# Spectral filter and squared-ReLU FFN: row means taken out in the residual sum, and an FFN norm without them

## The chip, the core and the metric

One core of one Trainium2 chip runs the whole program. The engines have their own instruction queues: TensorE (PE) multiplies, VectorE (DVE) and ScalarE (ACT) do elementwise work and move results from PSUM to SBUF, GpSimd (POOL) has a few jobs at the start, and SyncE (SP) issues most of the DMAs. The metric is the device time of one launch in microseconds; lower is better.

## The reference

The input is x of 2048 rows by 448 columns, in bf16. Two kinds of layer alternate, each twice:

```python
def _A_ref(x, w_r, w_i):                     # spectral filter
    X = rfft2(x.astype(float32))             # over the 2048 rows and 448 columns
    return irfft2(X * (w_r + 1j * w_i), s=(S, D)).astype(bfloat16)
def _B_ref(x, w1, b1, w2, b2):               # FFN, 448 -> 1792 -> 448
    r = maximum(x @ w1 + b1, 0)
    return (r * r) @ w2 + b2
x = A_x
x = x + _A_ref(layernorm(x), A_w_r, A_w_i)
x = x + _B_ref(layernorm(x), B_w1, B_b1, B_w2, B_b2)
x = x + _A_ref(layernorm(x), A_w_r, A_w_i)
x = x + _B_ref(layernorm(x), B_w1, B_b1, B_w2, B_b2)
```

The layer norm subtracts the row's mean and divides by sqrt(variance + 1e-5); it has no scale or offset of its own.

## The kernel before

**Tiles.** x stays in SBUF (`x_sb`, bf16) as 16 tiles of 128 rows. Weights and DFT matrices are loaded once. PSUM has eight banks of 512 fp32 columns; a tile of the program uses one bank or two neighbouring ones.

**The order of the work.** A planner (`_Sched`) collects all operations with their dependences, takes an order for each engine that is written out by hand as lists of operation numbers (`ORDER`), and sets the semaphores. Costs in the planner (such as `(n + 61) / 1.2` ns for an eviction on ACT) matter only where the order leaves a choice. `EV` says which engines may do an eviction. Where PE would stand still, the planner puts in filler matmuls on a matrix of ones (`warm_mm`, L1352).

**First spectral layer.** For each tile: row statistics on DVE or ACT, `rstd` (L865), then a DFT matrix scaled by rstd (`Fs`, L712 on POOL or DVE) and five matmuls (`first_A`), with one eviction into `XA`. Half of the input is first copied on POOL with a shift (`VT<-xin`, L701). Then `spectral`, in eight blocks p: `stage_TD` (matmuls on XA), `stage_B` (matmuls with G), `stage_W` (the complex multiply by the filter: chains of tensor_tensor on DVE, L729), and `stage_Bi` (matmuls with H, evicted into `VT` in single banks, two a block). After that `ffn` begins with the last step of the inverse transform: `stage_TI` (VT by TI, evicted to `tmp` as one instruction a group of one or two tiles) and `stage_AI` (tmp by FI), whose result is added to the residual by a scalar_tensor_tensor (STT, L1104): PSUM times 1.0 plus x, with the row's sum as a second output (`accum_out`).

**FFN norm.** `ln_B` squares x on ACT with a row sum (L1128). From the sum and the sum of squares come mean and variance by small DVE operations. Tiles 0 to 3 go into the FFN unnormalised: x is transposed (tiles 0 and 1 by matmuls with the flip matrix J, `flip`; 2 and 3 by a DMA transpose), and beside the 448 columns of x there are eight auxiliary columns: standard deviation and mean of the row, each as two bf16 parts (`cp` L733, `tt` L729). Their partners are extra rows of W1: b1 and minus the column sums of W1 over 448. So (x - mean) W1 + std b1 comes out of one matmul, relu and square are taken, and the second matmul's result is multiplied by rstd squared (`r2`) when it is added (L1245). Those column sums are made on the chip by `w1_aux` (L806 to L826): 16 matmuls of W1 with ones, an ACT copy scaled by -1/448, an STT for the rest (L820), and three DMAs into rows of W1, with two more for b1. Tiles 4 to 15 (`ln_rows`) are normalised before (`affine`: times rstd, plus -mean rstd, L721 and L722, which wait for small STTs at L1167 and L1171), transposed by DMA, and take b1 as the bias of the relu.

**FFN.** `h_part` and `h_pairs` do the first matmul, relu (ACT) and square (DVE, L729); `o_tile` the second matmul and the STT at L1245, which adds `xb` (x plus b2, a tensor_tensor done before). In the first FFN each finished tile goes on at once to the second spectral layer: `ln_stats` (bn_stats L834, bn_aggr L835), the fold x(d) +- x(447-d) and a second fold on DVE, the subtraction of the mean from one quarter (L738), `second_A` (four matmuls of 128 columns, one eviction to `XA`). The last tile is cut into two halves of 224 columns (`CUT`), the output's last into 336 and 112 (`CUT2`).

**Second spectral layer and second FFN** repeat this with folded matrices; the last STT writes the output tile.

Of the kernel before, what the change touches and what calls it, by code (L numbers as in the profile page):

```python
# [5 lines left out]
ACT = mybir.ActivationFunctionType  # L6
# [5 lines left out]
P = 128  # L12
S = 2048
D = 448
# [10 lines left out]
VB_PAIRS = (2, 3, 4, 5)  # L25

# [9 lines left out]
def make_constants():  # L36
# [88 lines left out]
1384 1389 1394 1399 1410 1404 1407 1413 1416""",  # L125
    "act": """
# [12 lines left out]
1306 1308 1303 1170 1171 1174 1177 1178 1377 1372 1370 1380 1375 1387 1382 1385 1392 1390 1397 1395 1400 1402""",  # L139
    "dve": """  # L140
# [26 lines left out]
    "pool": """  # L167
12 17 14 15 16 20 13 19 22 21 52 60 76 25 105 68 92 84 141 144 23 115 118 24 157 154 18""",
    "sp": """
3 6 4 10 36 8 30 28 41 29 33 32 31 45 34 27 39 37 46 40 44 38 163 35 164 165 166 167 332 355 376 379 378 399 421 442  # L170
401 463 1050 1073 1094 1096 1117 1138 1268 1265 1097 1274 1362 1159 1180 1318 1365 1359 1315 1368 1271 1406 1412 1312
1409 1321 1415 1418""",
}
# [1257 lines left out]
```

## Time and profile before

The runs took 269.94 us (median of three, 269.8 to 269.97).

| | |
|---|---|
| profiled execution | 269.8 us |
| its span | 267.9 us |
| PE busy | 256.9 us, 96% |
| DVE busy | 203.7 us, 76% |
| ACT busy | 175.6 us, 66% |
| POOL busy | 14.9 us, 6% |
| granted PE clock | 1.00 |

PE is busy nearly throughout. A busy PE in the table is a matmul in flight: matmuls overlap, so a row's duration is longer than the time it takes from the next. In the timeline a row is start, duration, engine, line, operation, output and inputs, sizes, count; the bracket at the end is the idle time before it and what ended it.

### The profile page before, as it was taken

Reading aid. Unit: us, or ns where it says so; the run is one execution under the profiler, and the core shown is the slowest. Engines: PE = TensorE matmul, PEld = TensorE weight load, DVE = VectorE, ACT = ScalarE, POOL = GpSimd, SP = SyncE. Lnnn points to the kernel's source line nnn. Section 1 sums busy time; section 2 is a strip of 40 time slices with the busy share of each in tenths; the row PEclk is TensorE's granted clock in tenths of the full one; section 3 lists DMA queues with packets and bytes.
Section 4 is the critical chain, followed back from the end, with each engine's and each line's share of the span. In section 5 each row is a group of like instructions: output and inputs, shape, how many; then the busy total and the mean of one; then the engine's idle time right before and its main releaser. Section 6 shows DMA issues by size and latency. Waiting matters only on the chain.

```text
span 267.9 us, 5691 instructions
## 1 busy us (share of the span) xinstructions
PE 256.9 (96%) x2090; PEld 165.1 (62%) x2090; DVE 203.7 (76%) x724; ACT 175.6 (66%) x393; POOL 14.9 (6%) x31
## 2 busy tenths in 40 slices
PE   8789998999999999999998998899999999999996
PEld 3667587778544555655567766688654675554454
DVE  3978996999999976299997899689995059734442
ACT  5977899987279746784226897899445885040930
POOL 8940000000000000000000000000000000000000
PEclk9999999999999999999999999999999999999999
DMA  7999410022300215000000000001423100023103
GB/s 232 404 291 347 157 40 1 3 40 42 66 10 20 41 22 107 4 0 2 1 0 2 2 0 0 4 14 30 78 60 68 42 0 0 20 39 92 52 0 103
DMA packets 25554, 16.33 MB, mean 61 GB/s; under 512 B 18186, under 2 KB 24566, under 8 KB 25528
## 3 DMA queue, kind: packets, MB, share of 16 engines
q1 hardware_dynamic: 24792, 14.26, 19.7%
q10 hardware_dynamic: 576, 0.92, 0.9%
q0 software_dynamic: 160, 0.81, 0.7%
q8 instruction: 16, 0.26, 0.4%
q14 instruction: 10, 0.08, 0.1%
HBM read 10.46 MB, written 1.84 MB: 46 GB/s over the span
## 4 chain that ended last, share of the span: by engine, by line
PE 76%; DVE 11%; ACT 7%; POOL 2%; issue 2%; DVEq 0%; ACTq 0%; POOLq 0%
PE ps L675 76%; ACT VT L700 4%; DVE tmp L729 4%; DVE arena L729 2%; DVE x_sb L1104 1%; ACT arena L700 1%; POOL Wt L772 1%; DVE x_sb L1245 1%; ACT arena L694 1%; DVE VT L729 1%; ACT XA L700 1%; DVE st L834 1%; POOL VT L701 1%; POOL W_sb L742 1%; ACT VT L1128 0%
## 5 line engine op out<-in xcount | busy, mean ns | idle before, releaser
L675 PE MATMUL ps<-yT,W_sb 64*128 64x512 bf16 (+1 forms) x770 | 90.2, 346 | 0.1
L675 PE MATMUL ps<-W_sb,arena 128*128 128x448 bf16 (+3 forms) x476 | 87.1, 342 | 0.0
L675 PEld LDWEIGHTS ps<-yT,W_sb 64*128 64x128 bf16 (+1 forms) x770 | 56.2, 95 | 30.3 <-ACT arena L694 1.6
L675 PEld LDWEIGHTS ps<-W_sb,arena 128*128 128x128 bf16 x476 | 45.5, 98 | 38.5 <-DVE arena L729 1.6
L729 DVE TENSOR_TENSOR arena<-arena 128x512 bf16<-128x512 bf16 (+1 forms) x140 | 45.2, 365 | 25.3 <-ACT arena L694 24.9
L694 ACT ACTIVATE arena<-ps,b1col 128x512 bf16<-128x512 f32 x84 | 51.7, 692 | 18.1 <-PE ps L675 17.9
L1128 ACT ACTIVATE VT<-x_sb 128x448 bf16<-128x448 bf16 x32 | 18.5, 581 | 22.4 <-DVE x_sb L1104 22.4
L700 ACT ACTIVATE arena<-ps 128x448 bf16<-128x448 f32 (+1 forms) x42 | 26.2, 723 | 6.0 <-PE ps L675 5.9
L1245 DVE SCALAR_TENSOR_TENSOR x_sb<-ps,arena 128x448 bf16<-128x448 f32 (+3 forms) x26 | 14.7, 582 | 12.5 <-PE ps L675 12.2
L694 ACT ACTIVATE mv<-mv,epst 128x1 f32<-128x1 f32 (+1 forms) x41 | 11.7, 296 | 16.9 <-DVE mv L835 10.8
L700 ACT ACTIVATE XA<-ps 128x512 bf16<-128x512 f32 x28 | 15.3, 594 | 6.0 <-PE ps L675 5.9
L694 ACT ACTIVATE arena<-ps 128x256 bf16<-128x256 f32 x56 | 17.8, 400 | 1.3 <-PE ps L675 1.3
L675 PE MATMUL ps<-arena,G_sb 128*128 128x448 bf16 (+1 forms) x84 | 17.0, 335 | 0.4 <-ACT arena L700 0.4
L675 PE MATMUL ps<-H_sb,arena 128*128 128x256 bf16 x128 | 16.2, 273 | 1.2 <-DVE arena L729 0.8
L675 PE MATMUL ps<-yT,VT 64*128 64x512 bf16 x42 | 15.8, 376 | 0.0
L700 ACT ACTIVATE VT<-ps 128x512 bf16<-128x512 f32 (+1 forms) x30 | 14.5, 631 | 1.4 <-PE ps L675 1.4
L729 DVE TENSOR_TENSOR tmp<-arena,Wt 128x896 bf16<-128x896 bf16 x26 | 14.8, 622 | 0.4 <-ACT arena L700 0.4
L675 PEld LDWEIGHTS ps<-H_sb,arena 128*128 128x128 bf16 x128 | 11.9, 98 | 5.1 <-DVE arena L729 3.3
L700 ACT ACTIVATE tmp<-ps 128x896 bf16<-128x896 f32 (+1 forms) x18 | 14.1, 850 | 1.4 <-PE ps L675 1.4
L675 PE MATMUL ps<-TD_sb,XA 112*128 112x112 bf16 (+1 forms) x184 | 13.9, 229 | 1.0 <-ACT XA L700 1.0
L675 PEld LDWEIGHTS ps<-TD_sb,XA 112*128 112x128 bf16 (+1 forms) x184 | 12.3, 98 | 2.8 <-DVE XA L701 1.2
L1104 DVE SCALAR_TENSOR_TENSOR x_sb<-ps,x_sb 128x448 bf16<-128x448 f32 x16 | 9.8, 620 | 4.5 <-PE ps L675 4.5
(89 smaller groups left out, 295.4 us busy)
## 6 DMA issues: line engine op xcount, KB each, us to landing
out_dram<-x_sb SPq DMA_DIRECT2D x15, 112.0 KB, 1.8
W_sb<-in_B_w_dram SPq DMA_DIRECT2D x1, 1568.0 KB, 10.1
W_sb<-in_B_w_dram SPq DMA_DIRECT2D x1, 1344.0 KB, 10.3
xin<-in_A_x_dram ACTq DMA_DIRECT2D x4, 224.0 KB, 4.8
xin<-in_A_x_dram SPq DMA_DIRECT2D x4, 224.0 KB, 4.2
H_sb<-c_H SPq DMA_DIRECT2D x1, 896.0 KB, 9.4
G_sb<-c_G SPq DMA_DIRECT2D x1, 672.0 KB, 7.9
Wt<-in_A_w_i_dram SPq DMA_DIRECT2D x1, 393.8 KB, 7.3
```

Of the source, the lines that this page charges most:

```text
L675: return sch.add("pe", lambda e: e.matmul(_res(o), lhsT, rhs, start=start, stop=stop, skip_group_check=skip), [lhsT, rhs], [o], cost=cost, ...
L694: sch.add("act", lambda e: e.activation(o, _res(i), func, **kw), rd, [o], cost=c)
L700: op = sch.add(engs[0], lambda e: e.activation(o, _res(i), ACT.Copy) if h[0].eng == "act" else e.tensor_copy(o, _res(i)), [i], [o], cost=c ...
L701: e.tensor_copy(o, _res(i)), [i], [o], cost=c[engs[0]], unit=unit)
L729: sch.add(eng, lambda e: e.tensor_tensor(o, _res(a), b, op), [a, b], [o], cost=_free(o) / rate + 69.0)
L742: sch.add(eng, lambda e: e.memset(o, v), [], [o], cost=_free(o) / 1.92 + 60.0)
L772: sch.add("pool", lambda e: e.indirect_dma_start(o, None, (A_w_r, A_w_i)[i], bass.IndirectOffsetOnAxis(ix[:], 0)), [ix[:]], [o], is_dma=Tr ...
L834: small(lambda e, si=si, xi=xi: e.bn_stats(si, xi), [xi], [si], _free(xi) / 0.96 + 69.0)
L1104: small(lambda e, xx=xx, xi=xi, r=r, i=i: e.scalar_tensor_tensor(out=xx, in0=_res(r), scalar=1.0, in1=xi, op0=ALU.mult, op1=ALU.add, accum ...
L1128: sch.add("act", lambda e, i=i, o=o, x=x: e.activation(o, x, ACT.Square, accum_out=sd[:, i, 1:2]), [x], [o, sd[:, i, 1:2]], cost=560.0)
L1245: small(lambda e: e.scalar_tensor_tensor(out=o, in0=_res(i), scalar=r[0] if r else 1.0, in1=xb[:, t, d0:d1], op0=ALU.mult, op1=ALU.add), [ ...
```

## The change

- **Mean in the residual sum.** The STT of `stage_AI` becomes PSUM minus mean plus x, with the mean of the row (known from the layer norm before) as a pointer scalar; it has no row sum any more. A filter of mean-free rows gives mean-free rows, so x in `x_sb` is mean-free after it, and the sum of squares alone gives the variance. Mean of the first norm (`mv`) and of the third (`mv2`, new) are added up into `mv2[..., 3]`, and given back in the last FFN: for tiles 0 to 3 as an STT in place of the tensor_tensor with b2 (`with_b2`), for the others in the STT of `o_tile`, by a pointer.
- **FFN norm.** Mean squared, variance and -mean rstd go. The square root follows the sum of squares. Two auxiliary columns (the standard deviation in two parts) remain of eight; `affine` becomes `scaled` (times rstd alone). `w1_aux` goes with its 16 matmuls and five DMAs; b1 goes twice into W1's extra rows by one DMA.
- **Evictions.** Blocks 1 to 5 of `stage_Bi` (`MERGE`) use two neighbouring banks and one instruction of 1,024 elements. `stage_TI` for tiles 0 and 1 uses two half tiles, evicted by ACT or DVE. The squares of tiles 0 and 1 may be done on DVE.
- **Last tile** of the first FFN: `o_tile` in two halves made of quarters (0, 3) and (1, 2), so that the fold can be done after each; `second_A` in two halves with eight matmuls of 64 columns and two evictions.
- **Order.** Costs of ACT in the planner go from 61 and 112 to 78 and 128, and all of `ORDER` is written anew. Among others, the memset of `x_sb` on POOL moves behind the copies, the b1 matmul moves from the start of the kernel into the first FFN, and for tiles 0 to 3 the second part of h follows the first without output matmuls between. Instructions: PE 2,092 to 2,078, DVE 694 to 652, ACT 361 to 353.

```diff
+MERGE = (1, 2, 3, 4, 5)
...
-        def w1_aux():
-            q = _Tile(1)
-            u = sch.new_unit("pe", 32)
-            for blk in range(4):
-                for i in range(4):
-                    mm(q[lambda b, i=i: ps[32 * i:32 * i + 32, b, 0:D]], ones[:, 0:32], W1_sb[:, blk, D * i:D * (i + 1)],
-                       blk == 0, blk == 3, skip=True, unit=u)
...
         def stage_Bi(p, first):
+                m = _Tile(2) if p in MERGE else None
...
+                if m:
+                    evac(VT[:, :, :, :, 2 * p:2 * p + 2, :].rearrange("p a g t c j -> p (a g t) (c j)"),
+                         m[lambda b: ps[:, b:b + 2, :].rearrange("p a (t c) -> p (a t) c", c=16)], EV["Bi"])
...
         def stage_TI(t, n, late):
+            if n == 1:
+                for g in range(2):
+                    q = _Tile(1)
+                    for r in range(2):
+                        mm(q[lambda b: ps[:, b, 0:HD]], VT[0:QD, r, g, t].rearrange("p c j -> p (c j)"), TI_sb[:, r, g, :],
+                           r == 0, r == 1)
+                    evac(TIo[:, t, g, :], q[lambda b: ps[:, b, 0:HD]], EV["TI1"])
+                return
...
-                small(lambda e, xx=xx, xi=xi, r=r, i=i: e.scalar_tensor_tensor(
-                    out=xx, in0=_res(r), scalar=1.0, in1=xi, op0=ALU.mult, op1=ALU.add, accum_out=sd[:, t + i, 0:1]),
+                m = (mv if first else mv2)[:, t + i, 0:1]
+                small(lambda e, xx=xx, xi=xi, r=r, m=m: e.scalar_tensor_tensor(
+                    out=xx, in0=_res(r), scalar=m, in1=xi, op0=ALU.subtract, op1=ALU.add), [r, xi, m], [xx], 545.0)
...
-            tt(u, a, a, ALU.mult)
...
-            small(lambda e: e.scalar_tensor_tensor(out=u, in0=a, scalar=-1.0 / D, in1=r, op0=ALU.mult,
-                                                   op1=ALU.mult), [a, r], [u])
             for i in range(n):
-                affine(xn[:, i, 0:D], x_sb[:, t + i, 0:D], rstd[:, t + i, 0:1], sd[:, t + i, 2:3], EV["XN"])
+                scaled(xn[:, i, 0:D], x_sb[:, t + i, 0:D], rstd[:, t + i, 0:1], EV["XN"])
...
+        def with_b2(t, n, last):
+            if t < 4 and last:
+                for i in range(t, t + n):
+                    m = mv2[:, i, 3:4]
+                    small(lambda e, i=i, m=m: e.scalar_tensor_tensor(out=xb[:, i, :], in0=x_sb[:, i, 0:D], scalar=m, in1=b2row[:],
+                                                                     op0=ALU.add, op1=ALU.add),
...
+            rs = [r2[:, t, 0:1]] if t < 4 else [mv2[:, t, 3:4]] if last else []
...
-        CUT = ((0, HD), (HD, D)) if HALVES else ((0, D),)
+        CUT = (lambda a: a.rearrange("p (k d) -> p k d", k=4)[:, 0:4:3], lambda a: a[:, QD:3 * QD])
...
+        def fold(t, d0, d1):
+            w = xin[:, t, :].rearrange("p (g d) -> p g d", g=2)
+            a, b = x_sb[:, t, d0:d1], x_sb[:, t, D - 1 - d0:D - 1 - d1:-1]
+            tt(w[:, 0, d0:d1], a, b, ALU.add)
+            tt(w[:, 1, d0:d1], a, b, ALU.subtract)
```

More of the change, by code (lines that the diff above doesn't have):

```diff
@@ L1121, in flip, with ln_B @@
                  EV["T"])
-        def ln_B(t, n):
+        def ln_B(t, n, last):
             for i in range(t, t + n):
@@ L1127, in ln_B @@
                 x = x_sb[:, i, 0:D].rearrange("p (a c) -> p a c", a=4)
[L1128 to L1129 removed]
+                h = []
+                op = sch.add("act", lambda e, i=i, o=o, x=x, h=h: e.activation(o, x, ACT.Square, accum_out=sd[:, i, 1:2])
+                             if h[0].eng == "act" else e.scalar_tensor_tensor(
+                                 out=o, in0=x, scalar=1.0, in1=x, op0=ALU.mult, op1=ALU.mult, accum_out=sd[:, i, 1:2]),
+                             [x], [o, sd[:, i, 1:2]], cost=575.0)
+                h.append(op)
+                if t < NFLIP:
+                    op.alt = {"act": 575.0, "dve": 545.0}
             if t >= 4:
[L1132 removed]
+                ln_rows(t, n, last)
                 return
[L1134 to L1136 removed]
+            b = sd[:, t:t + n, 1]
+            act(b, b, ACT.Sqrt, bias=epst[:, 0:1], scale=1.0 / D)
             if t < NFLIP:
[L1138 to L1149 removed]
+                flip(t, n, 0, 3)
+            aux = x_sb[:, t:t + n, D:D + 2]
+            cp(aux[:, :, 0], b)
+            tt(aux[:, :, 1], b, aux[:, :, 0], ALU.subtract)
             if t < NFLIP:
@@ L1156, in ln_B @@
             sch.tag = "xb" + sch.tag
-            tt(xb[:, t:t + n, :], x_sb[:, t:t + n, 0:D], b2row[:, None, :].to_broadcast([P, n, D]), ALU.add)
+            with_b2(t, n, last)
             small(lambda e: e.reciprocal(rstd[:, t:t + n, 0], b), [b], [rstd[:, t:t + n, 0]])
@@ L1179, in ln_rows @@
             sch.tag = "xb" + sch.tag
-            tt(xb[:, t:t + n, :], x_sb[:, t:t + n, 0:D], b2row[:, None, :].to_broadcast([P, n, D]), ALU.add)
+            with_b2(t, n, last)
             sch.bias += PR["xb"]
@@ L1235, in h_part, with o_tile, r @@
                 tt(hb, hb, hb, ALU.mult)
-        def o_tile(t, d0, d1):
+        def o_tile(t, cut, last):
             hb = hbuf[(t // 4) % 2]
             q = _Tile(1)
+            o, xi = cut(x_sb[:, t, 0:D]), cut(xb[:, t])
+            n = _free(o)
+            def r(a):
+                return a if len(list(o.ap)) == 2 else a.rearrange("p (k d) -> p k d", k=2)
             for fb in range(FB):
-                mm(q[lambda b: ps[:, b, 0:d1 - d0]], hb[:, fb, (t % 4) * P:(t % 4 + 1) * P], W2_sb[:, fb, d0:d1],
+                mm(q[lambda b: r(ps[:, b, 0:n])], hb[:, fb, (t % 4) * P:(t % 4 + 1) * P], cut(W2_sb[:, fb, :]),
                    fb == 0, fb == FB - 1)
-            o, i = x_sb[:, t, d0:d1], q[lambda b: ps[:, b, 0:d1 - d0]]
-            r = [r2[:, t, 0:1]] if t < 4 else []
-            small(lambda e: e.scalar_tensor_tensor(out=o, in0=_res(i), scalar=r[0] if r else 1.0, in1=xb[:, t, d0:d1],
-                                                   op0=ALU.mult, op1=ALU.add),
-                  [i, xb[:, t, d0:d1]] + r, [o], (d1 - d0) / 0.96 + 69.0)
+            i = q[lambda b: r(ps[:, b, 0:n])]
+            rs = [r2[:, t, 0:1]] if t < 4 else [mv2[:, t, 3:4]] if last else []
+            small(lambda e: e.scalar_tensor_tensor(out=o, in0=_res(i), scalar=rs[0] if rs else 1.0, in1=xi,
+                                                   op0=ALU.add if t >= 4 and last else ALU.mult, op1=ALU.add),
+                  [i, xi] + rs, [o], n / 0.96 + 69.0)
         def second_A(t):
@@ L1252, in second_A @@
             scaled(f, FA_sb[:, 0:P], rstd[:, t, 0:1], EV["FS2"])
-            q = _Tile(1)
+            n = 2 if t == NT - 1 else 1
+            q = [_Tile(1) for _ in range(n)]
+            w = P // n
+            u = sch.new_unit("pe")
             for k in range(2):
@@ L1313, in ffn @@
                     sch.bias, sch.tag = 5500.0 * (NT - t), f"o{L}.{t}"
-                    for d0, d1 in ((CUT2 if last else CUT) if t == NT - 1 else ((0, D),)):
-                        o_tile(t, d0, d1)
+                    for k, cut in enumerate((CUT2 if last else CUT) if t == NT - 1 else WHOLE):
+                        o_tile(t, cut, last)
                         if last:
-                            dma("sp", out_dram[:, t, d0:d1], x_sb[:, t, d0:d1])
+                            dma("sp", cut(out_dram[:, t, :]), cut(x_sb[:, t, 0:D]))
+                        elif t == NT - 1:
+                            fold(t, QD * k, QD * (k + 1))
                     if not last:
```

121 lines of the change are left out of this document (52 added, 69 removed), and 92 rows, old and new, of the table ORDER.

## The prediction

> **What bounds the kernel now.** I read the page's head and chain of waits first, then the windows of the stretches in which the chain leaves PE, then the timeline of PE around each of its gaps, with DVE, ACT, POOL and SP beside it.
>
> ```profile
> span 267.9 us, 5691 instructions
> PE 256.9 (96%) x2090; PEld 165.1 (62%) x2090; DVE 203.7 (76%) x724; ACT 175.6 (66%) x393; POOL 14.9 (6%) x31
> PE 76%; DVE 11%; ACT 7%; POOL 2%; issue 2%; DVEq 0%; ACTq 0%; POOLq 0%
> ```
>
> PE is busy for 96% of the span and carries 76% of the chain; DVE has 11%, ACT 7%. So an operation taken off DVE or ACT is worth something only where PE waits for it. Those places are few:
>
> ```profile
> 8.27 0.27 PE L675 MATMUL ps<-Fs,xin 128*128 128x256 bf16 x1 [1.43 <-POOL Fs L712]
> 14.85 0.27 PE L675 MATMUL ps<-Fs,m 128*128 128x256 bf16 x1
> 15.25 0.27 PE L675 MATMUL ps<-Fs,xin 128*128 128x256 bf16 x1
> 33.49 0.94 PE L675 MATMUL ps<-W_sb,ones 128*32 128x448 bf16 x16
> 34.36 0.61 PE L675 MATMUL ps<-H_sb,arena 128*128 128x256 bf16 x4
> 43.04 0.26 PE L675 MATMUL ps<-TI_sb,VT 112*128 112x224 bf16 x1 [0.49 <-DVE VT L701]
> 49.76 0.57 PE L675 MATMUL ps<-TI_sb,VT 112*128 112x112 bf16 x8 [0.43 <-ACT tmp L700]
> 143.86 0.61 PE L675 MATMUL ps<-Fs,tmp 128*128 128x128 bf16 x8 [0.52 <-DVE mv L835]
> 145.09 0.40 PE L675 MATMUL ps<-Fs,tmp 128*128 128x128 bf16 x4 [0.19 <-DVE tmp L738]
> 168.49 0.26 PE L675 MATMUL ps<-TI_sb,VT 112*128 112x224 bf16 x1 [0.46 <-DVE VT L701]
> 168.98 1.60 PE L675 MATMUL ps<-TI_sb,VT 112*128 112x224 bf16 x15 [0.23 <-ACT VT L700]
> 174.38 0.55 PE L675 MATMUL ps<-TI_sb,VT 112*128 112x112 bf16 x8 [0.62 <-DVE x_sb L733]
> ```
>
> The columns are start, duration, engine and line, tile, count, and in brackets the idle time with what ended it. The gaps lie in the start, at the two spectral-to-FFN joins (43 to 50, 168 to 175) and at the FFN-to-spectral join (143 to 146). The two W stretches are a mixed case, shown by their windows (length, then busy time of PE, PEld, DVE, ACT, POOL, granted clock, DMA):
>
> ```profile
> 20.00:42.00 22.00, 21.94 (x182) 15.78 (x180) 20.80 (x40) 19.24 (x36) 0.00 (x0) 1.00 0.51 167
> 149.40:167.00 17.60, 16.09 (x165) 11.80 (x162) 17.25 (x35) 16.08 (x28) 0.00 (x0) 1.00 0.00 1
> ```
>
> In the first W stretch PE and DVE are both full; in the second DVE is (17.25 of 17.60) and PE has 1.5 us of slack. The two FFN bodies (about 51 to 137 and 176 to 265) are PE's alone.
>
> **The change, part by part.**
>
> *Start.* The first real matmul waits for the scaled matrix Fs, made on POOL, and POOL's queue had a memset ahead of it, which now stands later:
>
> ```profile
> 5.85 0.31 POOL L742 MEMSET x_sb<- 128x256 bf16 x1
> 6.11 1.55 POOL L701 COPY VT<-xin 128x448 bf16<-128x448 bf16 x3
> 7.65 1.39 POOL L712 TENSOR_SCALAR Fs<-FA_sb,rstd 128x256 bf16<-128x256 bf16 x3
> ```
>
> Memset to next start is 6.11 - 5.85 = 0.26, so the first Fs can start at 7.39, and PE 0.26 earlier, if the statistics of that tile are there by then; they are DVE work of the first microseconds that is not lengthened. The tiles' order also differs, which can touch the gap of 15.25 - 14.85 - 0.11 = 0.29 (the 0.11 are 256 columns at the pace of the row at 168.98: (1.60 - 0.26)/14 = 0.096 us for 224). I take -0.35; ends 0 (the time is lost again at the stretch's last eviction) and -0.55.
>
> *Sums of W1 (w1_aux).* 16 matmuls go, 34.36 - 33.49 = 0.87 us of PE; so do one eviction on ACT, one STT on DVE and five small DMAs.
>
> ```profile
> 42.85 0.61 DVE L820 SCALAR_TENSOR_TENSOR yT<-ps,yT 128x448 bf16<-128x448 f32 x1
> ```
>
> The STT stands behind the evictions for which PE waits at 43.04, so it gives nothing. The 0.87 lie in the stretch where DVE is busy for 20.80 of 22.00: PE arrives earlier and waits for DVE's chain of complex multiplies. Ends 0 and -0.87; I take -0.05 for this and the new order of the stretch, because DVE's idle 1.2 us there is mostly its first wait and last evictions. What PE loses as cover is idle time, and nothing is queued behind it. On SP, the loads of the inverse DFT's and FFN's weights no longer stand behind the sums' DMAs; PE waits for none of them in the rows above, so 0.
>
> *Two-bank evictions of stage_Bi.* Five pairs a layer become single instructions.
>
> ```profile
> L700 ACT ACTIVATE VT<-ps 128x512 bf16<-128x512 f32 x26 | 13.4, 650 | 1.4 <-PE ps L675 1.4
> L700 ACT ACTIVATE arena<-ps 128x896 bf16<-128x896 f32 x16 | 14.1, 987 | 0.8 <-PE ps L675 0.8
> ```
>
> The slope (987 - 650)/384 = 0.88 ns an element gives 987 + 112 = 1100 ns for 1,024, against 2 x 650: up to 0.2 us of ACT a pair, 1 us a layer. The last pair's eviction starts later, since it waits for both banks, and the TI stage waits for VT by DVE first (0.49, 0.46). ACT is under its window in both W stretches; 0, ends -0.2 and +0.3 per layer.
>
> *First join (43 to 51).* Each residual STT loses its accumulator, and takes a pointer for a scalar in place of 1.0; the variance arithmetic (mean squared, subtraction, product with rstd) goes.
>
> ```profile
> L1245 DVE SCALAR_TENSOR_TENSOR x_sb<-ps,rstd,arena 128x448 bf16<-128x448 f32 x8 | 5.3, 677 | 0.0
> L1245 DVE SCALAR_TENSOR_TENSOR x_sb<-ps,arena 128x448 bf16<-128x448 f32 x22 | 13.2, 619 | 11.0 <-PE ps L675 10.7
> L1167 DVE SCALAR_TENSOR_TENSOR mv<-mv 128x2 f32<-128x2 f32 x12 | 1.8, 154 | 0.9 <-ACT VT L1128 0.7
> ```
>
> The pointer form is 677 - 619 = 58 ns dearer, on 32 STTs 1.9 us of DVE; some 44 small operations go, of which L1167's idle of 0.9 shows that they also waited on ACT. Along the join, PE does the same work, and its gap of 0.43 at 49.76 is an eviction on ACT, now two half ones of which DVE takes most. But the last FFN work on tiles 2 and 3 moves: the second h_part follows the first without the second output tile's matmuls between.
>
> ```profile
> 56.73 1.04 PE L675 MATMUL ps<-yT,W_sb 128*128 128x256 bf16 x8
> 57.60 2.81 PE L675 MATMUL ps<-W_sb,arena 128*128 128x448 bf16 x14
> 60.25 2.02 PE L675 MATMUL ps<-yT,W_sb 128*128 128x256 bf16 x17
> 55.55 1.34 SPq L662 DMA_TRANSPOSE yT<-x_sb  x1
> yT<-x_sb SPq DMA_TRANSPOSE x2, 3.0
> ```
>
> Before, the transpose of tiles 2 and 3 was issued at 55.55 and landed 3.0 later, and PE needed it at 60.25. Without the 14 output matmuls it is needed by about 57. By my count of what goes ahead of it, about nine small operations at some 0.15 in DVE's queue, the issue comes at about 54.2, the landing at 57.2: a wait of 0.2 to 0.5 may return what the join gains (0.2 to 0.4). I take -0.05, ends -0.4 and +0.9.
>
> *FFN bodies.* PE bound. The little matmul that turns b1 into a column moves from the start into this part; it takes no more than a 256-column one, so +0.11. DVE's longer STTs are covered by PE.
>
> *FFN-to-spectral join.* From the last half's STT to the last scaled product, DVE runs a chain of small operations:
>
> ```profile
> 142.72 0.38 DVE L1245 SCALAR_TENSOR_TENSOR x_sb<-ps,arena 128x224 bf16<-128x224 f32 x1
> 144.79 0.24 DVE L738 TENSOR_SCALAR tmp<-tmp,mv 128x112 bf16<-128x112 bf16 x1
> 146.24 1.73 PE L675 MATMUL ps<-TD_sb,XA 112*128 112x112 bf16 x32
> L738 DVE TENSOR_SCALAR tmp<-tmp,mv 128x112 bf16<-128x112 bf16 x16 | 3.8, 243 | 0.1
> L729 DVE TENSOR_TENSOR xin<-x_sb 128x224 bf16<-128x224 bf16 x32 | 7.8, 261 | 0.0
> ```
>
> Quarters let half of the fold go before the last STT; but folds of 112 elements cost nearly what those of 224 do (243 against 261), so the chain after it is about as long; four more matmuls of A2 add 4 x (0.40 - 0.22)/3 = 0.2 (x4 at 145.09, the last one's 0.22 off), and the last eviction, half as wide, returns 256 x 0.88 ns = 0.2. I take +0.05, ends -0.3 and +0.45 (4 x 243 - 2 x 261 = 450 ns, if both added folds come after the STT). Here the Trainium skill speaks against the change: "VectorE: DVE Perf Modes", its section on the TRN2 errata, says that each operation out of SBUF pays a fixed latency, that many small tiles pay it each time, and recommends at least 512 elements. The rows of 112 and 224 agree: half the elements save 18 ns. By its table (58 cycles at 0.96 GHz fixed) two more folds would be an estimated +0.12 in place of +0.05, the sum 0.07 later.
>
> *Second W stretch.* DVE is bound; its 35 instructions stay, in a new order that puts an independent multiply between some dependent ones. Of 17.60 - 17.25 = 0.35 idle I take 0.15 back; ends 0 and -0.35.
>
> *Second join (168 to 175).* Here h waits longest:
>
> ```profile
> 175.49 1.70 PE L675 MATMUL ps<-yT,W_sb 128*128 128x256 bf16 x14
> 173.60 0.62 DVE L1104 SCALAR_TENSOR_TENSOR x_sb<-ps,x_sb 128x448 bf16<-128x448 f32 x1
> 174.15 0.23 DVE L733 CAST x_sb<-mv 128x4 bf16<-128x4 f32 x2
> ```
>
> From the second TI matmul to h pass 6.51 us. The matmuls between have 12,448 columns, 5.3 us at 0.096 for 224; so up to 1.2 is idle, 0.62 of it in one wait for the aux columns (L733), which stood behind the STTs of tiles 2 and 3 (174.15 - 173.60 = 0.55 each). In the new order they stand ahead of them. What is late next is the square of tiles 2 and 3 and the added STTs for mean and b2 (four of 0.68, as L1245's pointer form), but those are wanted only by output tiles. I take one STT's time, -0.55, ends 0 and -1.2.
>
> *End.* The last STT takes a pointer: +0.06.
>
> Sum: -0.35 - 0.05 + 0 - 0.05 + 0.11 + 0.05 - 0.15 - 0.55 + 0.06 = -0.93. Against the profiled execution's 269.8 that is 268.9; the median of the runs, 269.94, stands 0.14 above it: 269.0.
>
> **The rivals.**
>
> B, a larger gain. In the first W stretch PE binds as much as DVE (21.94 of 22.00), and the 0.87 come off whole; with the start's other 0.2 that is 269.0 - 0.87 - 0.2 = 267.9. For it: PE's busy share is the higher. Against it: DVE's multiplies are one chain, and PE's busy time there holds waits.
>
> C, no change. The joins only shift their gaps: each engine arrives earlier and waits for the next one, as the gaps at 43.04 and 168.49 (both on evictions of VT) would not move. Then -0.05 - 0.15 + 0.11 + 0.05 + 0.06 and a third of the rest, -0.3: about 269.7.
>
> D, slower. The transpose of tiles 2 and 3 lands late in the first FFN. It decides once its issue is more than about 1.3 us later than my 54.2, that is at the old 55.5 or after: landing 58.5 against a need at 57, 1.5 us of PE, and none of the body's slack can return it: 269.0 + 1.5 = 270.5, more if the new order puts further DVE work ahead of it. Against it: the arithmetic before the transpose gets shorter.
>
> E, the clock falls. Fewer filler matmuls stand in the gaps; but the granted clock stayed at 1.00 even where PE was 18% idle:
>
> ```profile
> 160.00:170.00 10.00, 8.18 (x68) 5.93 (x66) 8.36 (x17) 8.01 (x18) 0.00 (x0) 1.00 0.00 1
> ```
>
> A stretch of 3 us at half the clock would cost 1.5: about 270.5.
>
> **How the numbers follow.** Forecast (268.4 to 269.4) 0.48; B 0.16; C 0.20; D 0.13; E 0.03. This kernel's runs can tell about 0.2%, 0.54 us, from no change, so "same" is 269.40 to 270.48. Faster: forecast and B and a little of C, 0.66; same: most of C and the milder D, 0.20; slower: the rest of D and E, 0.14. The range reaches from B's 267.9 with the second join's end (-0.5 more) to D: 267.4 to 270.6. The forecast's own is 268.4 to 269.4.
>
> **What would show it.** Right: the first Fs matmul at about 8.0; DVE's W chain of the first layer not shorter, PE idle in it; h of the second FFN 5.9 to 6.0 after its second TI matmul; the last A2 matmul to TD as before. Wrong: h of the first FFN broken by a wait on a DMA after 56 matmuls (D), a first TI matmul more than 0.7 earlier than the start explains (B), or the joins as long as before (C).

## The result and the profile after

The changed kernel takes 269.11 us (median of eight runs, 268.94 to 269.54) against 269.94: a ratio of 0.997 with a 95% interval of 0.9961 to 0.9979, about 0.8 us less. The forecast was 269.0. That it lies so near is in part luck: several of its terms were wrong, with opposite signs, and the runs below show which.

The profiled execution of the changed kernel was its slowest, 269.54 us, so its span is only 0.2 under that of before. The head of its page and its chain of waits:

```profile
span 267.7 us, 5562 instructions
PE 256.5 (96%) x2076; PEld 162.7 (61%) x2076; DVE 202.1 (75%) x653; ACT 175.8 (66%) x382; POOL 14.5 (5%) x30
PE 66%; DVE 22%; issue 2%; ACT 1%; DVEq 0%
```

PE's busy share is what it was. The chain's share of DVE went from 11% to 22%, that of ACT from 7% to 1%: the chain now leaves PE mostly for DVE. The timeline of PE, at the start of each stage and at its waits:

```profile
8.02 0.27 PE L674 MATMUL ps<-Fs,xin 128*128 128x256 bf16 x1 [0.62 <-POOL Fs L711]
15.38 0.27 PE L674 MATMUL ps<-Fs,xin 128*128 128x256 bf16 x1 [0.54 <-issue]
18.95 1.69 PE L674 MATMUL ps<-TD_sb,XA 128*128 128x224 bf16 x16 [0.89 <-ACT XA L699]
43.13 1.81 PE L674 MATMUL ps<-TI_sb,VT 112*128 112x224 bf16 x22 [0.46 <-DVE VT L700]
50.96 0.27 PE L674 MATMUL ps<-yT,W_sb 128*128 128x256 bf16 x1
...
66.92 0.60 PE L674 MATMUL ps<-yT,W_sb 128*128 128x256 bf16 x4
68.09 0.54 PE L674 MATMUL ps<-tmp,FI_sb 128*128 128x224 bf16 x4 [0.56 <-ACT arena L693]
...
146.83 1.73 PE L674 MATMUL ps<-TD_sb,XA 112*128 112x112 bf16 x32
169.00 1.88 PE L674 MATMUL ps<-TI_sb,VT 112*128 112x224 bf16 x24 [0.57 <-DVE VT L700]
174.99 2.78 PE L674 MATMUL ps<-yT,W_sb 128*128 128x256 bf16 x24
```

From the starts of the first matmul of each stage (Fs, TD, TI and h, twice) comes a table of stage lengths in us. It is the tool of all that follows, because all stages but one agree between profiles within some 0.05 where an edit does not reach them; the first, Fs to TD, does not.

| kernel | to Fs | Fs to TD | TD to TI | TI to h | h to TD | TD to TI | TI to h | h to end |
|---|---|---|---|---|---|---|---|---|
| before | 8.27 | 10.35 | 24.42 | 7.52 | 95.68 | 22.25 | 7.00 | 92.41 |
| after | 8.02 | 10.94 | 24.18 | 7.82 | 95.88 | 22.16 | 6.00 | 92.73 |
| e1_quarter_sums | 8.27 | 10.78 | 24.75 | 7.25 | 95.70 | 22.25 | 6.99 | 93.11 |
| e2_memset_late | 8.02 | 10.36 | 24.43 | 7.52 | 95.70 | 22.25 | 6.99 | 92.42 |
| e3_pool_apart | 8.02 | 9.81 | 24.19 | 7.82 | 95.88 | 22.17 | 5.99 | 92.73 |
| e4_fi_first | 8.02 | 10.57 | 24.18 | 7.82 | 95.31 | 22.16 | 5.99 | 92.73 |
| e5_quarter_sums_same_banks | 8.26 | 10.35 | 24.43 | 7.44 | 95.70 | 22.24 | 7.00 | 93.05 |
| e6_no_mean | 8.01 | 10.63 | 24.19 | 7.63 | 95.73 | 22.16 | 5.97 | 92.63 |
| e7_split_evictions | 8.01 | 10.70 | 24.18 | 8.11 | 95.88 | 22.17 | 5.99 | 92.73 |
| e8_columns_first | 8.27 | 10.34 | 24.42 | 7.52 | 95.68 | 22.26 | 7.78 | 94.60 |
| e9_three | 8.02 | 10.03 | 24.19 | 7.82 | 95.14 | 22.16 | 6.00 | 92.43 |
| e10_halves | 8.00 | 10.39 | 24.19 | 7.82 | 95.87 | 22.17 | 5.99 | 92.72 |
| e11_narrow_sums | 8.27 | 10.55 | 24.42 | 7.44 | 95.70 | 22.25 | 6.99 | 92.40 |
| e12_squares_on_act | 8.01 | 10.54 | 24.19 | 7.83 | 95.88 | 22.18 | 7.19 | 92.77 |

After against before: -0.25 to the first Fs, +0.59 in the first stage, -0.24 in the first W stretch, +0.30 at the first join, +0.20 in the first FFN, -0.09 in the second W stretch, -1.00 at the second join, +0.32 in the second FFN; together -0.17.

Most of the +0.59 belongs to this one execution. In it DVE stands 0.46 us for a load of the input:

```profile
11.69 1.16 DVE L818 BATCH_NORM_STATS2 st<-xin 128x6 f32<-128x448 bf16 x2 [0.46 <-DMA xin<-in_A_x_dram]
```

The profile of e10_halves, whose first stage is the same program, has no such wait, and there Fs to TD is 10.39; e4, e6, e7 and e12, with the same first stage, lie between. On the kernel before, e1 and e11 show a wait of the same kind (0.54 and 0.31) and 10.78 and 10.55 in place of 10.35. With 10.39 for the first stage, after against before is +0.04 there and -0.72 together, near the -0.83 of the medians.

### The profile page after: what moved, and what is told of

It is laid out like the page before. It is cut to its first block, busy times and chain, and to the rows that moved or that the text cites. A ratio compares the mean times of both kernels' runs of the same rounds, so it can differ in the third digit from the quotient of the medians.

```text
span 267.7 us, 5562 instructions
## 1 busy us (share of the span) xinstructions
PE 256.5 (96%) x2076; PEld 162.7 (61%) x2076; DVE 202.1 (75%) x653; ACT 175.8 (66%) x382; POOL 14.5 (5%) x30
## 4 chain that ended last, share of the span: by engine, by line
PE 66%; DVE 22%; issue 2%; ACT 1%; DVEq 0%
PE ps L674 66%; DVE tmp L728 10%; DVE arena L728 3%; DVE x_sb L1104 2%; DVE VT L728 1%; DVE st L818 1%; DVE x_sb L1250 1%; DVE xin L728 1%; DVE VT L700 1%; DVE VT L1129 1%; ACT arena L699 1%; PE ps L1373 0%; DVE Fs L711 0%; DVE tmp L737 0%; DVE yT L700 0%
## 5 line engine op out<-in xcount | busy, mean ns | idle before, releaser
L674 PEld LDWEIGHTS ps<-yT,W_sb 64*128 64x128 bf16 (+1 forms) x770 | 54.5, 95 | 32.1 <-ACT arena L693 1.7
L699 ACT ACTIVATE arena<-ps 128x448 bf16<-128x448 f32 (+1 forms) x42 | 26.9, 703 | 6.2 <-PE ps L674 6.1
L1128 ACT ACTIVATE VT<-x_sb 128x448 bf16<-128x448 bf16 x29 | 16.7, 579 | 13.3 <-DVE x_sb L1104 13.3
L693 ACT ACTIVATE mv<-mv,epst 128x1 f32<-128x1 f32 (+1 forms) x45 | 12.9, 296 | 16.2 <-DVE mv L819 16.0
L693 ACT ACTIVATE arena<-ps 128x256 bf16<-128x256 f32 x56 | 18.4, 399 | 3.3 <-PE ps L674 3.1
L699 ACT ACTIVATE XA<-ps 128x512 bf16<-128x512 f32 (+1 forms) x28 | 15.2, 584 | 7.7 <-PE ps L674 7.7
L1250 DVE SCALAR_TENSOR_TENSOR x_sb<-ps,mv,arena 128x448 bf16<-128x448 f32 (+2 forms) x13 | 8.1, 644 | 12.2 <-PE ps L674 12.1
L710 ACT ACTIVATE arena<-x_sb,rstd 128x448 bf16<-128x448 bf16 x12 | 7.8, 665 | 13.0 <-DVE x_sb L1250 7.0
L699 ACT ACTIVATE VT<-ps 128x1024 bf16<-128x1024 f32 (+2 forms) x20 | 14.1, 784 | 0.8 <-PE ps L674 0.8
L699 ACT ACTIVATE tmp<-ps 128x896 bf16<-128x896 f32 (+1 forms) x15 | 12.6, 880 | 1.5 <-PE ps L674 1.5
```

Source lines behind the costliest of these rows:

```text
L674: return sch.add("pe", lambda e: e.matmul(_res(o), lhsT, rhs, start=start, stop=stop, skip_group_check=skip), [lhsT, rhs], [o], cost=cost, ...
L693: sch.add("act", lambda e: e.activation(o, _res(i), func, **kw), rd, [o], cost=c)
L699: op = sch.add(engs[0], lambda e: e.activation(o, _res(i), ACT.Copy) if h[0].eng == "act" else e.tensor_copy(o, _res(i)), [i], [o], cost=c ...
L710: op = sch.add(engs[0], lambda e: e.activation(o, i, ACT.Copy, scale=s) if h[0].eng == "act" else e.tensor_scalar(o, i, s, 1.0, op0=ALU.mu ...
L1128: op = sch.add("act", lambda e, i=i, o=o, x=x, h=h: e.activation(o, x, ACT.Square, accum_out=sd[:, i, 1:2]) if h[0].eng == "act" else e.sc ...
L1250: small(lambda e: e.scalar_tensor_tensor(out=o, in0=_res(i), scalar=rs[0] if rs else 1.0, in1=xi, op0=ALU.add if t >= 4 and last else ALU. ...
```

## The experiments

**The sums of W1.** Does the first W stretch get shorter when PE has less to do? In the kernel before, only the first block of W1 is summed.

```diff
-            for blk in range(4):
+            for blk in range(1):
...
-                       blk == 0, blk == 3, skip=True, unit=u)
+                       blk == 0, blk == 0, skip=True, unit=u)
```

> The kernel before, with the sums of W1 cut from 16 matmuls to 4 (only the first block of W1 is summed, so the auxiliary rows hold a quarter of the sum; 12 matmuls, 0.65 us of PE, are left out). Theory 1 (DVE's chain of multiplies sets the first W stretch): PE idles instead, first TI matmul at 43.0 as before, time 269.9, within 0.15. Theory 2 (rival B, PE sets it): the first TI matmul 0.5 to 0.65 earlier, time 269.3 to 269.4.

Measured: 270.81 us, ratio 1.0027 (1.0017 to 1.0036): slower, which neither theory had. The smaller cost in the planner had given other PSUM banks to the last inverse matmuls (TD to TI is 24.75), so this run tells nothing on the question; its second FFN is 0.70 longer too, at the place that the next run shows. In the next the planner's cost is held (`x.cost *= 4` behind the matmul).

> As e1_quarter_sums (4 of the 16 matmuls of the sums of W1 left in the kernel before, so the auxiliary rows are a quarter of the sum), but with the planner's cost of these four held at that of the sixteen, so that every later PSUM tile keeps the bank that it has in the kernel before; e1 had other banks for the last inverse matmuls and a new wait of 0.48 at 39.65 on an eviction. Theory 1 (DVE's multiplies set the first W stretch): PE waits about 0.6 more for DVE, first TI matmul at 43.0, time 269.9 to 270.0. Theory 2 (PE sets it): first TI matmul 0.5 to 0.65 earlier, time 269.3 to 269.4.

Measured: 270.73 us, ratio 1.0035 (1.0022 to 1.0047). TD to TI is 24.43, as before: on the W stretch theory 1 holds, PE's 0.65 us are worth nothing there (and 0.08 from TI to h). But the second FFN is 0.64 longer, at one place. Rows of PE and DVE of this kernel, and its DMA queues between 198 and 205 us (packets, MB, share of 16 engines):

```profile
204.15 0.70 DVE L722 TENSOR_SCALAR arena<-x_sb,rstd,mv 128x448 bf16<-128x448 bf16 x2 [1.55 <-DMA yT<-arena]
205.45 0.82 PE L675 MATMUL ps<-yT,W_sb 64*128 64x512 bf16 x6 [0.30 <-DVE x_sb L1105]
```

```profile
q1 hardware_dynamic: 1056, 0.26, 20.0%
q14 instruction: 1, 0.01, 1.4%
q8 instruction: 1, 0.02, 0.8%
```

The same queues of the kernel before, in the same window:

```profile
q1 hardware_dynamic: 1056, 0.26, 19.7%
q14 instruction: 1, 0.01, 0.3%
```

A load of instructions (queue 8) falls on the DMA transpose of two tiles; the transpose lands late, DVE waits 1.55 us for the buffer that it reads from, and PE behind DVE. In e1 the packet lies there as well, and the same wait is 1.60. Is that a matter of where the instructions stand in PE's stream? The next kernel removes nearly the same PE time but no instruction.

```diff
+                    w = D if blk == 0 else 16
-                    mm(q[lambda b, i=i: ps[32 * i:32 * i + 32, b, 0:D]], ones[:, 0:32], W1_sb[:, blk, D * i:D * (i + 1)],
+                    x = mm(q[lambda b, i=i, w=w: ps[32 * i:32 * i + 32, b, 0:w]], ones[:, 0:32], W1_sb[:, blk, D * i:D * i + w],
...
+                    x.cost = D / 2.4 / 4
```

> The kernel before with all 16 matmuls of the sums of W1, 12 of them with 16 columns in place of 448 (so again only a quarter of the sum is made), the planner's costs as before: the same PE time goes as in e5_quarter_sums_same_banks, but every instruction keeps its place in PE's stream. Theory 1 (e5's loss of 0.57 at 204.8 came from a load of instructions that met a DMA transpose, since 12 instructions fewer shift these loads): no wait there, time 269.8 to 270.0. Theory 2 (it came from PE running ahead by the removed time): again 270.6 to 270.8.

Measured: 269.82 us, ratio 0.9998 (0.9989 to 1.0007). Its row for the same DVE operation:

```profile
203.00 0.70 DVE L722 TENSOR_SCALAR arena<-x_sb,rstd,mv 128x448 bf16<-128x448 bf16 x2 [0.19 <-DMA yT<-arena]
```

The wait is 0.19 in place of 1.55, and no packet of queue 8 is in the window. Theory 1 holds on both counts: the 12 of the 16 matmuls that these runs cut were all but free, and with 12 instructions fewer the kernel lost 0.8 us. That the load holds the transpose up is inferred from their meeting, in e1 and e5 and not here; no run moves the load alone.

**The start.** On GpSimd's order of the kernel before (unit 13 is the memset):

```diff
-12 17 14 15 16 20 13 19 22 21 52 60 76 25 105 ...
+12 17 14 15 16 20 19 22 21 52 60 76 25 13 105 ...
```

> The kernel before, with the memset of x_sb on GpSimd moved behind the first Fs tiles and one more copy. Theory 1: first Fs matmul at 8.0 in place of 8.27, and the start keeps it: TD begins near 18.35, time 269.65 to 269.7. Theory 2: the 0.25 are lost again before TD, since the last evictions of XA on ACT and DVE end the stage, not the first matmul: TD at 18.6, time 269.9.

Measured: 269.78 us, ratio 0.9995 (0.9986 to 1.0004). The profile shows theory 1: Fs at 8.02, TD at 18.37, 0.25 earlier, and the end as much earlier. The times show 0.2 in the median, less than the interval can tell from nothing.

So the memset's 0.25 is kept if nothing else changes. In the kernel after the stage behind it hides a loss. Rows of DVE and then of GpSimd in the kernel after, near the end of that stage:

```profile
14.57 0.90 DVE L711 TENSOR_SCALAR Fs<-FA_sb,rstd 128x256 bf16<-128x256 bf16 x2 [0.20 <-PE ps L674]
16.12 1.04 DVE L711 TENSOR_SCALAR Fs<-FA_sb,rstd 128x256 bf16<-128x256 bf16 x1
16.31 0.84 DVE L832 TENSOR_REDUCE m<-mv 128x2 bf16<-128x4 f32 x1
...
14.14 1.06 POOL L700 COPY VT<-xin 128x448 bf16<-128x448 bf16 x2
16.13 0.95 POOL L741 MEMSET arena<- 128x1024 bf16 x1
```

The Fs tile at 16.12 ends at 17.16, just after GpSimd's memset (17.08); the first of the two at 14.57 took 0.71 of the 0.90 and ended just after GpSimd's copies (15.20). These rows are as long in e10_halves (0.90, 1.04 and 0.84), so the late load is not their cause. The next kernel keeps them apart.

```diff
-... 24 116 119 129 132 13 25 26 155 18""",
+... 24 116 119 25 129 132 26 155 13 18""",
...
+        for k in (13, 18):
+            sch.units[k].ops[0].deps.append(sch.units[158].ops[0])
         sch.schedule()
```

> The kernel after, with GpSimd's work at the end of the first stage taken out of DVE's way: one copy goes into GpSimd's idle time before 13.0, and the two memsets wait until DVE's last Fs tile is done. Theory 1 (DVE's Fs tiles at 14.57 and 16.12 took 0.71 and 1.04 us in place of 0.29 because GpSimd's copy and memset ran at that time): these Fs tiles take 0.28, TD begins 0.4 to 0.8 earlier than at 18.95, time 268.4 to 268.8, and the runs spread less than the 268.94 to 269.54 of the kernel after. Theory 2 (these DVE tiles were long for another reason, such as late input): still 0.7 and 1.0, time 269.1.

Measured: 268.56 us (268.41 to 269.04), ratio 0.9946 (0.9933 to 0.9959). The same operations of DVE:

```profile
14.10 0.59 DVE L711 TENSOR_SCALAR Fs<-FA_sb,rstd 128x256 bf16<-128x256 bf16 x2 [0.20 <-PE ps L674]
...
15.33 0.28 DVE L711 TENSOR_SCALAR Fs<-FA_sb,rstd 128x256 bf16<-128x256 bf16 x1
15.53 0.15 DVE L832 TENSOR_REDUCE m<-mv 128x2 bf16<-128x4 f32 x1
```

The last Fs tile is back at 0.28 and the first, which meets the end of a copy, at 0.35; Fs to TD is 9.81, 0.58 under e10_halves. Theory 1 holds, 0.55 us in the medians; only the spread of the runs did not get smaller, as I had expected. The input's loads fit that: e9_three, which has this move too, shows a wait of 0.27 for one at 11.55 and 10.03.

**PE's new wait in the first FFN.**

```diff
-... 500 506 509 361 497 380 524 554 ...
+... 500 506 509 361 380 497 524 554 ...
```

> The kernel after, with one group of four FI matmuls of the first FFN (tiles 10 and 11, at 68.09, where PE waited 0.56 for a relu) moved ahead of the last four matmuls of h before it. Theory 1 (this wait is for the PSUM banks that those four matmuls of h use, a price of the new order): no wait there, time 268.5, 0.5 to 0.6 less than after. Theory 2 (PE catches up later, so the wait is free, or the FI group waits for its own input instead): 269.0 to 269.1.

Measured: 268.57 us, ratio 0.9941 (0.9928 to 0.9953). PE's rows there:

```profile
66.18 0.93 PE L674 MATMUL ps<-tmp,FI_sb 128*128 128x224 bf16 x8
66.94 0.60 PE L674 MATMUL ps<-yT,W_sb 128*128 128x256 bf16 x4
67.38 2.81 PE L674 MATMUL ps<-W_sb,arena 128*128 128x448 bf16 x14
```

The wait is gone, h to TD falls from 95.88 to 95.31, and nothing takes its place there. The planner's own list agrees: it puts this group into banks 2 and 3, and bank 3 held those four matmuls of h. Theory 1 holds: one swap in the order was worth 0.54.

**The pointer scalar.**

```diff
-                    out=xx, in0=_res(r), scalar=m, in1=xi, op0=ALU.subtract, op1=ALU.add), [r, xi, m], [xx], 545.0)
+                    out=xx, in0=_res(r), scalar=0.0, in1=xi, op0=ALU.subtract, op1=ALU.add), [r, xi, m], [xx], 545.0)
```

> The kernel after, with the residual STT's pointer replaced by the constant 0.0, so that the row mean is not subtracted there (it is left out; the end still adds it). Theory 1 (a pointer scalar costs 0.058 us each, and only the two joins feel it): the 32 STTs take 0.62 in place of 0.68, time 269.0 to 269.1, at most 0.2 less than after. Theory 2 (the pointer is what holds the gain down): 268.5 or less.

Measured: 268.74 us, ratio 0.9957 (0.9944 to 0.9971), 0.37 under the kernel after. Groups of the kernel after, then of this one (count, busy time, mean ns):

```profile
L1104 DVE SCALAR_TENSOR_TENSOR x_sb<-ps,mv,xin 128x448 bf16<-128x448 f32 x16 | 10.5, 675 | 0.3 <-PE ps L674 0.3
```

```profile
L1104 DVE SCALAR_TENSOR_TENSOR x_sb<-ps,xin 128x448 bf16<-128x448 f32 x16 | 9.5, 617 | 0.3 <-PE ps L674 0.3
```

The price of one is 58 ns, as forecast from another line. What it costs in all lies between the two theories: TI to h 7.82 to 7.63, h to TD 95.88 to 95.73, the second FFN 92.73 to 92.63. At 58 ns each that is six to eight of the 32 on the path, not the one that I had counted.

**The two-bank evictions**, undone in the same banks: in place of one `evac` of 1,024 elements, two of 512 in one unit.

```diff
-                    evac(VT[:, :, :, :, 2 * p:2 * p + 2, :].rearrange("p a g t c j -> p (a g t) (c j)"),
-                         m[lambda b: ps[:, b:b + 2, :].rearrange("p a (t c) -> p (a t) c", c=16)], EV["Bi"])
+                    u = None
+                    for k in range(2):
+                        u = evac(VT[:, k, :, :, 2 * p:2 * p + 2, :],
+                                 m[lambda b, k=k: ps[:, b + k, :].rearrange("p (g t c j) -> p g t c j", g=2, t=16, c=2)], EV["Bi"], u)
...
```

> The kernel after, with each of the ten two-bank evictions of the inverse step undone into two of one bank each, in the same banks and order. Theory 1 (ACT is under cover in both W stretches): time within 0.2 of after, 269.0 to 269.3, ACT 0.2 us longer per pair. Theory 2 (ACT's queue matters there): 269.8 to 270.5, PE waits on ACT in 30 to 43 and 155 to 168. Below nothing is possible too: the second half's eviction no longer holds back the first half's data, 268.8.

Measured: 269.39 us, ratio 0.9978 (0.9969 to 0.9987), 0.28 over the kernel after, a difference as large as each interval's half width. The profile has it at one place: TI to h is 8.11 in place of 7.82.

```profile
42.90 0.26 PE L674 MATMUL ps<-TI_sb,VT 112*128 112x224 bf16 x1 [0.34 <-ACT VT L699]
43.57 1.43 PE L674 MATMUL ps<-TI_sb,VT 112*128 112x224 bf16 x21 [0.41 <-ACT VT L699]
```

With split evictions PE waits for ACT here, where in the kernel after it waits for DVE (0.46 at 43.13). So ACT was not under cover at the end of the first W stretch; at the second join nothing changed (5.99).

**The last tile's quarters**, undone (`CUT` into left and right halves, one fold of two operations after the second half):

```diff
-        CUT = (lambda a: a.rearrange("p (k d) -> p k d", k=4)[:, 0:4:3], lambda a: a[:, QD:3 * QD])
+        CUT = (lambda a: a[:, 0:HD], lambda a: a[:, HD:D])
...
-                        elif t == NT - 1:
-                            fold(t, QD * k, QD * (k + 1))
+                        elif t == NT - 1 and k == 1:
+                            fold(t, 0, HD)
```

> The kernel after, with the last tile of the first FFN cut into its left and right halves again, and its fold done in two operations of 224 after the second half, in place of four of 112. In the trace of after only one of the four folds of 112 stands ahead of the second half's STT. Theory 1 (quarters save nothing, because folds of 112 cost nearly what those of 224 do): within 0.1 of after, 269.0 to 269.2, from the last STT to TD 3.5 to 3.6 us in both. Theory 2 (they save half a fold): 0.2 slower. Theory 3 (they cost the fixed time of two more operations): 0.1 to 0.2 faster.

Measured: 269.10 us, ratio 0.9975 (0.9963 to 0.9986). The last half's STT and the first TD matmul of this kernel, and the STT of the kernel after:

```profile
142.74 0.39 DVE L1250 SCALAR_TENSOR_TENSOR x_sb<-ps,arena 128x224 bf16<-128x224 f32 x1
146.28 1.73 PE L674 MATMUL ps<-TD_sb,XA 112*128 112x112 bf16 x32
```

```profile
143.29 0.39 DVE L1250 SCALAR_TENSOR_TENSOR x_sb<-ps,arena 128x224 bf16<-128x224 f32 x1
```

3.54 us in both (146.28 - 142.74, 146.83 - 143.29): quarters are worth nothing and cost nothing. Theory 1 holds in its time, but not in its reason. From start to next start a fold of 112 takes 0.10 to 0.12 us here and one of 224 takes 0.14 to 0.18; the three small ones behind the last STT and the two large ones come to 0.32 alike.

**The second join.** First the order, in the kernel before (unit 1042 is the STT of tile 3):

```diff
-1010 1041 1042 1014 1031 1032 1015 1013 1056 1034 1017 1057 ...
+1010 1041 1014 1031 1032 1015 1013 1056 1034 1017 1042 1057 ...
```

> The kernel before, with the second FFN's residual STT of tile 3 moved behind the auxiliary columns of tiles 0 and 1 in DVE's order, and nothing else. Theory 1 (the gain of the second join, 7.00 to 6.00 us from TI to h, is the order): the columns start at 173.8 in place of 174.15, h comes 0.3 to 0.4 earlier, 6.6 to 6.7 from TI to h. Theory 2 (the gain is the fewer small operations and the square on DVE): h comes as before, 7.0. The total can lose it again, since the planner gives other banks and four more fillers from there on: 269.5 to 270.2.

Measured: 272.88 us, ratio 1.0114 (1.0099 to 1.013). The columns did start at 173.84, but h did not come earlier; TI to h is 7.78. PE's rows:

```profile
174.67 0.57 PE L675 MATMUL ps<-TI_sb,VT 112*128 112x112 bf16 x8 [0.71 <-ACT tmp L700]
...
185.83 0.39 PE L675 MATMUL ps<-yT,W_sb 128*128 128x256 bf16 x2 [1.11 <-DMA yT<-x_sb]
```

Both theories fall. A TI matmul reads nothing of the auxiliary columns; what it can wait for is a PSUM bank. In the kernel before, the planner gives this group the two banks that the STTs of tiles 2 and 3 read, so the 0.62 at 174.38 was the wait for the second of them, whose row runs from 173.60 to 174.22, and the operation that the row names had merely come next. My edit delayed that very STT; the planner then took other banks, and those are freed by evictions on ACT. The second row is rival D's mechanism, in the second FFN: the STT of tile 3 came later, the transpose was issued later, and PE stood 1.11 us for it. The added fillers and other banks are part of the 3 us as well, so this run's total is not explained to the last part.

New theory: what counts at this join is what ACT has to do between its evictions. (The expectation below says that e8 showed this of the wait in the kernel before as well. It did not; it showed it of its own.) The squares of tiles 0 and 1, which the changed kernel does on DVE, go back to ACT:

```diff
 act:  -... 1029 970 968 996 985 1011 1049 991 ...
       +... 1029 970 967 968 996 984 985 1011 1049 991 ...
 dve:  967 and 984 leave the list
```

> The kernel after, with the squares of tiles 0 and 1 in the second FFN moved from DVE to ACT, as they are in the kernel before, each ahead of its square root in ACT's order. e8_columns_first showed that PE's wait at the second join (0.62 at 174.38) is for ACT's evictions to tmp, ahead of which ACT did two squares and two roots, not for the auxiliary columns. Theory 1 (the gain of the second join, 7.00 to 6.00 us from TI to h, comes from ACT being free of the squares): 6.5 to 7.0 again, time 269.6 to 270.1. Theory 2 (it comes from the fewer small operations and the new order): 6.0 to 6.2, time 269.1 to 269.3.

Measured: 270.45 us, ratio 1.0018 (1.0008 to 1.0028), 1.34 over the kernel after; TI to h is 7.19. ACT and PE of this kernel:

```profile
172.54 0.60 ACT L1128 ACTIVATE VT<-x_sb 128x448 bf16<-128x448 bf16 x1
173.47 0.90 ACT L699 ACTIVATE tmp<-ps 128x896 bf16<-128x896 f32 x1
174.26 0.56 ACT L1128 ACTIVATE VT<-x_sb 128x448 bf16<-128x448 bf16 x1
175.15 1.70 ACT L699 ACTIVATE tmp<-ps 128x896 bf16<-128x896 f32 x2
...
174.00 0.23 PE L674 MATMUL ps<-J_sb,x_sb 128*128 128x128 bf16 x1 [0.26 <-DVE x_sb L728]
174.42 0.93 PE L674 MATMUL ps<-tmp,FI_sb 128*128 128x448 bf16 x4 [0.18 <-ACT tmp L699]
```

and ACT's evictions in the kernel after, with only a root between them:

```profile
173.20 0.92 ACT L699 ACTIVATE tmp<-ps 128x896 bf16<-128x896 f32 x1
174.01 0.28 ACT L693 ACTIVATE mv<-mv,epst 128x1 f32<-128x1 f32 x1
174.20 1.71 ACT L699 ACTIVATE tmp<-ps 128x896 bf16<-128x896 f32 x2
```

Each square puts about 0.7 us between two evictions of ACT (0.6, its sum's 0.2 partly beside it, and the wait for its root). What h waits for behind them is no bank. PE's waits above are for the auxiliary columns (0.26) and for ACT's eviction to tmp (0.18), which its FI matmuls read; and the root follows the square, and the columns follow the root. DVE and PE of this kernel, then PE of the kernel after:

```profile
173.59 0.16 DVE L732 CAST x_sb<-mv 128x1 bf16<-128x1 f32 x1 [1.17 <-ACT mv L693]
175.28 0.16 DVE L732 CAST x_sb<-mv 128x1 bf16<-128x1 f32 x1 [0.87 <-ACT mv L693]
175.75 0.23 PE L674 MATMUL ps<-J_sb,x_sb 128*128 128x128 bf16 x1
```

```profile
174.94 0.22 PE L674 MATMUL ps<-J_sb,x_sb 128*128 128x128 bf16 x1
```

That last flip matmul takes the columns of tile 1, and h starts 0.07 behind it. So here the columns are on the path, as the prediction had them, but late by ACT's queue and not by the STTs of tiles 2 and 3. Theory 1 holds for this order of the work: with the two squares on ACT it loses 1.2 us, more than the whole gain of this join. It does not follow that the squares are worth 1.2 against the kernel before, which has them on ACT and takes 7.00: another order may suit them better than this one, with 7.19.

**A faster version.** The kernel after with e3's and e4's edits, and one more swap in the second FFN (`1016 1156` becomes `1156 1016`):

> The kernel after with three moves together: GpSimd's work out of DVE's way (as e3_pool_apart), the FI group of tiles 10 and 11 ahead of the last h matmuls (as e4_fi_first), and in the second FFN the FI group of tiles 4 and 5 behind one more group of h, where PE waited 0.35 for DVE at 180.6. If the gains of e3 (0.55) and e4 (0.54) are of separate places, they add: 269.1 - 0.55 - 0.54 = 268.0, and up to 0.4 less with the third move, 267.6. If both are the same slack seen twice, 268.5.

Measured: 267.47 us (267.36 to 267.61), ratio 0.9907 (0.9892 to 0.9922). The gains add, and the third swap brings 0.3 (h to end 92.73 to 92.43): 2.4 us under the kernel before, three times what the change itself brought.

## Why the prediction was right or wrong

- **Start, -0.35: right in sign, too large.** The first Fs matmul came at 8.02, as said (-0.25). The stage behind it is 10.39 against 10.35 when the input comes in time (e10), so the start gained 0.21. What failed is that I saw only the order's gain: without the clash (e3) the stage is 9.81, 0.54 under before, but the new order put GpSimd's copies and a memset on DVE's Fs tiles, which took all of it back (0.58), a loss that I had not looked for.
- **Sums of W1, 0: right** as far as tried (e5, e11); rival B falls. The stretch got 0.24 shorter all the same, against the 0.05 that I gave to its order; which part of the order did it was not tried.
- **Two-bank evictions, 0: mis-sized.** Undoing them costs 0.28 at the first join and nothing at the second. ACT's window being under full (19.24 of 22.00) did not mean that its last evictions were covered.
- **First join and first FFN, -0.05 and +0.11: wrong.** Measured +0.30 and +0.20. The +0.30 is work moved: a group of four FI matmuls, 0.39 to the next row, that stood behind the start of h (at 54.50) now stands ahead of it (at 50.47). From TI to TD it is +0.50 in all, and -0.07 without one wait (e4, 103.13 against 103.20), near the +0.06 forecast. I had put the wait at the start of the second part of h, near 57, on the transposes. They were in time (the issue came at 53.85, against 54.2 forecast); PE waited at that part's end, at 68.09, 0.56 for PSUM banks, since four matmuls of h held what the FI group behind them needed (e4). The b1 matmul is at 62.03, 0.11 ahead of the next, as sized.
- **FFN-to-spectral join, +0.05: right** in size (3.52 to 3.54 us from STT to TD), in part by luck. I had compared two operations, a tensor_scalar of 112 (243 ns) and a tensor_tensor of 224 (261); among the folds themselves the small ones are cheaper, and one of the four stands ahead of the STT (e10). The advice of the Trainium skill on small tiles ("VectorE: DVE Perf Modes", the TRN2 errata), which spoke against the change, made no difference that the times show: quarters and halves take the same.
- **Second W stretch, -0.15: right in sign**, 0.09.
- **Second join, -0.55: right in sign, wrong in cause.** -1.00 there, of which the second FFN returned 0.32 in one new wait of 0.35, which the third swap of e9 takes away. Of the 1.00, 0.23 lies between the first two TI matmuls (0.49 apart before, 0.26 after): the sum had it at nothing, and no run shows what took it away. The other 0.77 stands against the -0.55. "0.62 of it in one wait for the aux columns" is the step that failed: I took the releaser's name from the row, though the waiting matmul reads nothing of it; it waited for the banks of tile 3's STT. And the new order could gain only because two squares had left ACT's queue (e12), which I had not counted at all.
- **Pointer scalars, +0.06 at the end only: mis-sized.** The 58 ns each were right; they cost 0.37 in all (e6).

Stage by stage, with the first stage as in e10, the kernel came out against the forecast: 0.14 slower in the start, 0.19 faster in the first W stretch, 0.39 slower from there to the second TD, 0.06 slower in the second W stretch, and 0.19 faster from the second join to the end. That leaves 0.2, and 0.1 in the medians. The total was right by luck in so far as two losses that I had not seen, GpSimd's and the bank wait, of about 0.55 each, were nearly made up by gains that I had not seen either.

## What to carry to other kernels

When an order is written anew, look for the places where two engines or two PSUM users now meet, not only at what the edits remove: here two such places cost more than the whole change gained, and small moves in the order won them back. Look at a second profile of the same program before you explain a stage: most of the +0.59 in the first stage was a late load in one execution. Before believing the releaser of a wait, ask whether the waiting operation reads anything that the named one writes; for a matmul that reads nothing of it, look for the PSUM bank. Move small work off the engine whose queue holds what PE waits for, even onto the busier engine: in this order two squares on DVE in place of ACT were worth 1.2 us, and 12 matmuls cut from PE nothing.

## What the runs showed of the hardware

- A DVE tensor_scalar from SBUF to SBUF (128x256, bf16) took 0.28 us alone, and 0.71 and 1.04 while GpSimd ran a copy or a memset (0.56 and 0.95 long); it ended 0.08 after GpSimd's operation each time, and the small reduction queued behind it showed 0.84 in place of 0.15. The Trainium skill, "SBUF — State Buffer", section "Who interferes with whom", says that the two engines share a pair of ports which one of them holds for a whole instruction while the other stands still; the trace agrees. It also names tensor_reduce as never in contention on trn2; the 0.84 here is of one behind a blocked operation, so it neither agrees nor disagrees.
- The place of instructions in an engine's stream can cost time: with 12 matmuls fewer, a load of instructions of 0.02 MB met a DMA transpose, and DVE waited 1.55 us for it (e5; 1.60 in e1) in place of 0.19; time +0.8 us with less work. That the one holds up the other is inferred.
- A pointer in place of a constant makes an STT of 128x448 out of PSUM 58 ns longer (675 against 617).
